# A mirrored hidden sum made on VectorE instead of by two more matmuls

## The chip, the cores and the metric

The kernel runs on one core of a Trainium2 chip. The metric is the device time of one execution in microseconds (us); the time before is the median of three executions. A core has five engines with a queue each, and a queue is worked off in order: TensorE (PE in the profile, its weight loads PEld), VectorE (DVE), ScalarE (ACT), GpSimd (POOL) and SyncE (SP). They are tied together by semaphores only, so an instruction that waits holds up all that stands behind it on its engine.

## The reference

```
X = np.fft.fft(x, axis=1)            # x: 8 x 3008 x 256, over the sequence
X = np.fft.fft(X, axis=2).real       # over the 256 features
h = np.maximum(X.reshape(24064, 256) @ w_in, 0.0)     # w_in: 256 x 2048
out = (h * h) @ w_out                                  # w_out: 2048 x 256
```

## The kernel before

**The algebra.** The feature transform and `w_in` are multiplied once, into `gh` (128 x 3 x 2048, f16): `gh[:,0]` for the cosine rows, `gh[:,1]` for the sine rows. The sequence transform of each batch is folded by its symmetries (`fold_steps`) and multiplied with tables into `zc` and `zs` (`z_steps`, lines 520 to 587): 128 rows, one column for each frequency. With P = `gh[:,0]`ᵀ·`zc` and Q + N = `gh[:,1]`ᵀ·`zs`, the full sum P+Q+N is the hidden layer at a frequency k, and P−Q+N is the one at the mirrored frequency. N is what row 0 of `zs` adds: the sine of feature frequency 0 is zero, and that row carries the cosine row of d = 128 instead, which does not change sign. `gh[:,2]` is `gh[:,1]` times −2, with row 0 set to 0 (`turn2`, line 329), so that adding `gh[:,2]`ᵀ·`zs` to the full sum turns it into P−Q+N.

**Windows and steps.** The 8 x 1505 = 12040 frequency columns are cut into 25 windows `w` of 512 columns (the first six 240, 512, 512, 240, 512, 448, the last 360; the others 512; `w` counts from 0). Each window has 8 steps `s` of two 128-row chunks of the 2048 hidden features. A step's order in the code (lines 774 to 786) is:

1. `pq(s)`: four matmuls of 512 columns into the PSUM tile `ph` (lines 742 and 743), giving P+Q+N for both chunks;
2. `square(s, 0)`: ScalarE takes the ReLU of `ph` into `h1` (line 757), VectorE squares it into `h2` (line 759);
3. `others(s)`: side work spread over the steps. It holds 16 matmuls of 256 columns of the second layer of the window before (line 647), whose results ScalarE copies out in every odd step (line 662); fold work on VectorE, one piece a step; and the z matmuls of the windows to come (line 540) with ScalarE's copies (lines 545 and 551) and VectorE's `minus` (line 563);
4. `turn(s)`: two matmuls that add `gh[:,2]`ᵀ·`zs` to the same `ph` (line 748);
5. `square(s, 1)`: ReLU and square again, columns reversed, for the mirrored half.

PSUM is full: `ph` has two buffers of two banks, the second layer's `po` two banks, `pz` two.

**What else is where.** Six windows (w = 5, 8, 10, 13, 16, 19; `fold_at`) hold the folds of a batch: `d_even` to `odds` in steps 0 to 4, `even` in step 6, `back` in step 7, each with much VectorE work (lines 410 to 437). In them GpSimd issues the load of the next batch (lines 125 and 130, step 2), the store of the even half to DRAM (line 439, step 6) and its four reads back (lines 447 and 449, step 7), which wait for that store to land. Six windows (w = 6, 9, 12, 15, 18, 21; `late_at`) hold the `late` pieces on VectorE: `fold8` twice (line 463, steps 2 and 3) and `fold16` twice (line 474, steps 4 and 5). Batch columns begin at such places that z matmuls lie in the windows 4, 6, 7, 9, 10, 11, 13, 14, 16, 17, 19, 20 and 22. The order on every engine is the order of the code: `manual_schedule` (line 98).

Of the kernel before, what the change touches and what calls it, by code (L numbers as in the profile page):

```python
# [7 lines left out]

F32 = mybir.dt.float32
F16 = mybir.dt.float16  # L10
I32 = mybir.dt.int32
AF = mybir.ActivationFunctionType
ALU = mybir.AluOpType

HS = 32.0
P = 128
# [12 lines left out]
def kernel(  # L29
# [14 lines left out]
    nc = tc.nc  # L44
    B, S, D = x.shape
    _, F = moe_w_in.shape
# [7 lines left out]
    NFC = F // P  # L54
    WN = 512
# [7 lines left out]
    NE = E + 1  # L63
# [15 lines left out]
    NW = len(wins)  # L79
# [25 lines left out]
    zp = ctx.enter_context(tc.tile_pool(name="zp", bufs=4))  # L105
    h1p = ctx.enter_context(tc.tile_pool(name="h1p", bufs=3))
    h2p = ctx.enter_context(tc.tile_pool(name="h2p", bufs=2))
    osp = ctx.enter_context(tc.tile_pool(name="osp", bufs=3))
    drp = ctx.enter_context(tc.tile_pool(name="drp", bufs=2, space=bass.MemoryType.DRAM))
    ps_h = ctx.enter_context(tc.tile_pool(name="ps_h", bufs=2, space=bass.MemoryType.PSUM))  # L110
# [43 lines left out]
    def iota(shape, pattern, base, mult, name):  # L154
        t = const.tile(shape, I32, name=name)
        nc.gpsimd.iota(t, pattern=pattern, base=base, channel_multiplier=mult)
        return t
# [9 lines left out]
        idx["r"] = iota([P, 1], [[1, 1]], P - 1, -1, "idx_r")  # L167

    xs = {0: load_x(0, idx_first)}
    w16 = [const.tile([P, 2, F // 2], F16, name=f"w16_{i}") for i in range(2)]  # L170
    for i in range(2):
        nc.gpsimd.dma_start(out=w16[i], in_=moe_w_in[:, i * F // 2 : (i + 1) * F // 2].rearrange("(c p) f -> p c f", p=P))
    wout16 = const.tile([P, NFC, D], F16, name="wout16")
# [4 lines left out]
    perm = [const.tile([P, P], F16, name=f"perm{i}") for i in range(2)]  # L178
    for i in (1, 0):
        nc.gpsimd.tensor_scalar(out=perm[i], in0=prow_i, scalar1=float(P - 1 - i), scalar2=None, op0=ALU.is_equal)  # L180
    evec_i = iota([P, 2], [[1, 2]], 0, 2, "evec_i")
    idx["c"] = iota([P, 1], [[1, 1]], P - 1, -1, "idx_c")
    nc.gpsimd.memset(idx["c"][0:2, :], P - 3)
# [39 lines left out]
    def table_steps(e):  # L223
# [17 lines left out]
                i += cnt  # L241

        def args(h):
            t = st["t", h] = tmp.tile([P, 3, NE], F32, name="t", tag="tt")
            for j in range(nr):
                r = row(h, j)
                if e == 0:
                    nc.scalar.activation(t[:, j, 0:n], st["kf"], AF.Copy, bias=R23, scale=vs[:, r : r + 1])
                else:
                    nc.vector.tensor_scalar(out=t[:, j, 0:n], in0=st["kf"], scalar1=vs[:, r : r + 1], scalar2=R23, op0=ALU.mult, op1=ALU.add)  # L250
# [237 lines left out]

    def gh_scale(out, pg, act):
        if act:  # L490
            nc.scalar.activation(out, pg, AF.Copy, bias=0.0, scale=1.0 / HS)
        else:
            nc.vector.tensor_scalar(out=out, in0=pg, scalar1=1.0 / HS, scalar2=None, op0=ALU.mult)  # L493

    def gh_step(cc, act=None):

# [11 lines left out]
    def gh_turn(cc):  # L508
        f0 = cc * 512
        nc.vector.tensor_scalar(out=gh[:, 2, f0 : f0 + 512], in0=gh[:, 1, f0 : f0 + 512], scalar1=turn2[:, 0:1], scalar2=None, op0=ALU.mult)  # L510

    zc, zs = {}, {}

# [172 lines left out]
    for i in range(2, B):  # L686
        fold_at[win_of(col_of[i, 0]) - 2] = i
        late_at[win_of(col_of[i, 1]) - 2] = i
    NST = NFC // 2
    old = None  # L690
    for w in range(NW):
        g0, wn = wins[w]
# [45 lines left out]
        def pq(s):  # L738
            ph = phs[s] = ps_h.tile([P, 2, 512], F32, name="ph", tag="psh")
            for a in range(2):  # L740
                f0 = (2 * s + a) * P
                nc.tensor.matmul(ph[:, a, 0:wn], gh[:, 0, f0 : f0 + P], zcw[:, 0:wn], start=True, stop=False)  # L742
                nc.tensor.matmul(ph[:, a, 0:wn], gh[:, 1, f0 : f0 + P], zsw[:, 0:wn], start=False, stop=True)  # L743

        def turn(s):
            for a in range(2):
                f0 = (2 * s + a) * P
                nc.tensor.matmul(phs[s][:, a, 0:wn], gh[:, 2, f0 : f0 + P], zsw[:, 0:wn], start=False, stop=True, skip_group_check=True)  # L748

        def square(s, sg):  # L750
            h1 = h1p.tile([P, 2, 512], F16, name="h1", tag="h1")
            if w == 1 and not sg:

                for a in range(2):
                    nc.scalar.activation(h1[:, a, 0:wn], phs[s][:, a, 0:wn], AF.Relu)  # L755
            else:
                nc.scalar.activation(h1[:, :, 0:wn], phs[s][:, :, 0:wn], AF.Relu)  # L757
            hv = rev_dim(h1[:, :, 0:wn], 2) if sg else h1[:, :, 0:wn]
            nc.vector.tensor_tensor(h2[:, 2 * s : 2 * s + 2, sg * wn : (sg + 1) * wn], hv, hv, op=ALU.mult)  # L759

        def others(s):
            for j in at[s]:
                j()
            for j in spread(f2, s, NST):
                j()
            for j in post[s]:
                j()
            if s == lo:
                zl[:] = [j for zu, part, h in zj for j in zu(part, h)]
            if s >= lo:  # L770
                for j in spread(zl, s - lo, hi - lo) if s < hi else []:
                    j()

        ng = 2 if w == 0 else 1
        for s0 in range(0, NST, ng):
            ss = range(s0, s0 + ng)
            for s in ss:
                pq(s)
            for s in ss:
                square(s, 0)  # L780
            for s in ss:
                others(s)
            for s in ss:
                turn(s)
            for s in ss:
                square(s, 1)
        old = (w, h2)
    for j in ffn2_steps(*old, tail=True):
        j()
# [30 lines left out]
```

## Time and profile before

| | us |
|---|---|
| device time, median of 3 (641.11, 641.24, 641.28) | 641.24 |
| span of the profiled execution, first to last instruction | 639.3 |
| PE busy, 4550 instructions | 617.4 (97%) |
| ACT busy, 618 | 456.5 (71%) |
| DVE busy, 609 | 372.5 (58%) |
| POOL busy, 130 | 77.0 (12%) |

The page gives no device time for the profiled execution alone; about 1.9 us of the median lie outside its span. The busy times of the four engines are of one execution and overlap. Matmuls are pipelined: the time that one is shown with is longer than the distance to the next. The granted TensorE clock is 0.997 over the span.

### The profile page before, as it was taken

The page shows a single profiled execution, that of the slowest core. Times are in us where ns is not written, and L with a number is a line of the kernel's source. Part 1 is how long each engine was busy: PE and PEld are TensorE (multiplying, and loading weights), DVE is VectorE, ACT ScalarE, POOL GpSimd, SP SyncE. Part 2 cuts the span into 40 slices and gives each one's busy share as a digit, 9 for nine tenths or more (in the row PEclk, how much of TensorE's full clock was granted, in tenths as well). Part 3 has the DMA queues.
Part 4 walks back from the last instruction along what each step waited for, and adds up shares of the span by engine and source line. Part 5 has one row for each costly group of instructions (what it writes and reads, how often), then busy time and mean ns, then how long its engine had stood idle before and what let it go on. Part 6 is the DMA issues. An engine that isn't in the chain of part 4 may idle for free.

```text
span 639.3 us, 11596 instructions
## 1 busy us (share of the span) xinstructions
PE 617.4 (97%) x4550; PEld 439.3 (69%) x4550; DVE 372.5 (58%) x609; ACT 456.5 (71%) x618; POOL 77.0 (12%) x130
## 2 busy tenths in 40 slices
PE   5789999999999999999999999999999999999997
PEld 2456686676676767777677667776777767776786
DVE  7777755675546656745566455764558545544440
ACT  6677766876777767777777677777777777677762
POOL 8202220012000220220003100022000200000000
PEclk9999999999999999999999999999999999999999
DMA  8736321154111721631116411173111311111112
GB/s 151 116 80 139 103 90 34 32 107 127 49 34 46 162 82 34 125 112 52 36 50 120 122 35 49 40 152 87 45 26 58 108 35 37 48 44 36 49 54 66
DMA packets 36540, 47.52 MB, mean 74 GB/s; under 512 B 4231, under 2 KB 30343, under 8 KB 36487
## 3 DMA queue, kind: packets, MB, share of 16 engines
q0 software_dynamic: 9344, 22.14, 17.2%
q1 hardware_dynamic: 26915, 24.44, 12.5%
q8 instruction: 35, 0.57, 0.4%
q10 hardware_dynamic: 228, 0.21, 0.1%
q14 instruction: 18, 0.15, 0.1%
HBM read 33.63 MB, written 27.84 MB: 96 GB/s over the span
## 4 chain that ended last, share of the span: by engine, by line
PE 91%; ACT 3%; DVE 3%; issue 2%; POOL 0%; ACTq 0%; POOLq 0%; DVEq 0%
PE po L647 50%; PE ph L748 12%; PE ph L743 12%; PE ph L742 12%; PE pz L540 4%; ACT h L757 2%; PE pw L314 1%; DVE h L759 1%; ACT h L755 0%; PE pg L503 0%; DVE gh L493 0%; ACT cos L277 0%; DVE fe L410 0%; DVE fo L414 0%; ACT osb L662 0%
## 5 line engine op out<-in xcount | busy, mean ns | idle before, releaser
L757 ACT ACTIVATE h<-ph 128x1024 f16<-128x1024 f32 (+3 forms) x392 | 361.2, 975 | 85.7 <-PE ph L748 78.9
L759 DVE TENSOR_TENSOR h<-h 128x1024 f16<-128x1024 f16 (+3 forms) x400 | 262.3, 660 | 230.1 <-ACT h L757 222.9
L647 PE MATMUL po<-wout,h 128*128 128x256 f16 (+1 forms) x3024 | 361.6, 273 | 0.0
L647 PEld LDWEIGHTS <-h 128*128 128x128 f16 (+1 forms) x3024 | 296.5, 98 | 71.5
L742 PE MATMUL ph<-zc,gh 128*128 128x512 f16 (+3 forms) x400 | 146.2, 368 | 2.7 <-ACT h L757 1.3
L743 PE MATMUL ph<-zs,gh 128*128 128x512 f16 (+3 forms) x400 | 146.2, 368 | 0.9 <-DVE zs L563 0.7
L748 PE MATMUL ph<-zs,gh 128*128 128x512 f16 (+3 forms) x400 | 114.0, 367 | 5.0 <-ACT h L757 3.1
L662 ACT ACTIVATE osb<-po 128x512 f32<-128x512 f32 (+2 forms) x94 | 54.9, 587 | 59.6 <-PE po L647 54.8
L743 PEld LDWEIGHTS <-gh 128*128 128x128 f16 x400 | 39.2, 98 | 46.4 <-issue 3.8
L742 PEld LDWEIGHTS <-gh 128*128 128x128 f16 x400 | 39.3, 98 | 44.0 <-issue 2.0
L748 PEld LDWEIGHTS <-gh 128*128 128x128 f16 x400 | 37.2, 98 | 15.4 <-issue 7.9
L480 POOL COPY xy<-xy 128x2 f16<-128x2 f16 x16 | 2.5, 186 | 164.6 <-DVE xy L463 164.6
L125 POOL DMA_DIRECT2D xo<-in_x_dram x8 | 6.1, 762 | 122.7 <-DVE fo L414 112.2
L130 POOL DMA_INDIRECT xo<-in_x_dram,idx_r x15 | 18.7, 1246 | 4.5 <-issue 4.3
L545 ACT ACTIVATE es<-pz 128x376 f32<-128x376 f32 (+1 forms) x32 | 15.4, 481 | 4.4 <-PE pz L540 2.8
L449 POOL DMA_INDIRECT rb<-scr,idx_r x16 | 17.9, 1120 | 4.9 <-issue 4.9
L551 ACT ACTIVATE zs<-pz 128x376 f16<-128x376 f32 (+22 forms) x26 | 8.3, 362 | 9.7 <-PE pz L540 9.7
L314 PE MATMUL pw<-spn 128*128 128x384 f16 x32 | 7.8, 409 | 6.7 <-DVE spn L308 6.7
L563 DVE SCALAR_TENSOR_TENSOR zc<-es,pz 128x376 f16<-128x376 f32 (+22 forms) x27 | 9.4, 383 | 7.3 <-ACT zc L551 7.3
L563 DVE SCALAR_TENSOR_TENSOR zs<-es,pz 128x376 f16<-128x376 f32 (+22 forms) x27 | 9.4, 383 | 7.1 <-ACT zs L551 7.1
L439 POOL DMA_DIRECT2D scr<-ev x8 | 4.7, 589 | 70.1 <-DVE ev L437 63.0
L540 PE MATMUL pz<-sin,od 128*128 128x376 f16 x48 | 12.2, 322 | 0.6 <-ACT es L545 0.6
(116 smaller groups left out, 245.2 us busy)
## 6 DMA issues: line engine op xcount, KB each, us to landing
out_dram<-osb SPq DMA_DIRECT2D x77, 128.0 KB
xo<-in_x_dram POOLq DMA_DIRECT2D x7, 768.0 KB, 6.7
scr<-ev POOLq DMA_DIRECT2D x8, 390.0 KB, 4.0
rb<-scr POOLq DMA_DIRECT2D x16, 130.0 KB, 2.5
out_dram<-osb SPq DMA_DIRECT2D x12, 94.0 KB
w<-in_moe_w_in_dram POOLq DMA_DIRECT2D x2, 512.0 KB
wout<-in_moe_w_out_dram POOLq DMA_DIRECT2D x1, 1024.0 KB
out_dram<-osb SPq DMA_DIRECT2D x8, 75.0 KB
```

The costliest lines, as they stand in the source:

```text
L130: nc.gpsimd.indirect_dma_start(out=flat(q), out_offset=None, in_=bass.AP(tensor=x.tensor, offset=0, ap=[[XW, B * S * D // XW], [1, XW]]), ...
L449: nc.gpsimd.indirect_dma_start(out=rb[:, q].rearrange("p r d -> p (r d)"), out_offset=None, in_=bass.AP(tensor=src.tensor, offset=src.offs ...
L540: nc.tensor.matmul(ps[:, o0:o1], lhs, tab, start=(h == 0 and k == 0), stop=last, skip_group_check=True)
L545: nc.scalar.activation(es[:, 0:n], ps[:, 0:n], AF.Copy, bias=0.0, scale=1.0)
L563: nc.vector.scalar_tensor_tensor(out=zwin(w)[part][:, o : o + cnt], in0=es[:, a : a + cnt], scalar=2.0, in1=ps[:, a : a + cnt], op0=ALU.mu ...
L647: nc.tensor.matmul(po[0:m, j * D : (j + 1) * D], h2[:, fc, q : q + m], wout16[:, fc, :], start=(fc == 0), stop=(fc == NFC - 1))
L662: nc.scalar.activation(osb[0:mm].rearrange("p s d -> p (s d)")[:, lo:hi], po[0:mm, lo:hi], AF.Copy, bias=0.0, scale=HS * HS)
L742: nc.tensor.matmul(ph[:, a, 0:wn], gh[:, 0, f0 : f0 + P], zcw[:, 0:wn], start=True, stop=False)
L743: nc.tensor.matmul(ph[:, a, 0:wn], gh[:, 1, f0 : f0 + P], zsw[:, 0:wn], start=False, stop=True)
L748: nc.tensor.matmul(phs[s][:, a, 0:wn], gh[:, 2, f0 : f0 + P], zsw[:, 0:wn], start=False, stop=True, skip_group_check=True)
L757: nc.scalar.activation(h1[:, :, 0:wn], phs[s][:, :, 0:wn], AF.Relu)
L759: nc.vector.tensor_tensor(h2[:, 2 * s : 2 * s + 2, sg * wn : (sg + 1) * wn], hv, hv, op=ALU.mult)
```

## The change

- The scale of `gh` changes its sign, and ReLU gets the scale −1, so `ph` now holds the negated sums.
- From w = 4 on some steps are made in another way: steps 2, 4 and 6, or step 5 alone in windows with folds. There `cosines` makes −P alone (two matmuls), `twice` has VectorE compute `t2` = −2·`ph` + 2N = 2P + 2N into SBUF, `sines` adds −(Q+N) (two matmuls, after `others`), ScalarE takes the ReLU of the full sum as before, and VectorE makes the mirrored half as max(`t2` + `ph`, 0) with a custom instruction (`TENSOR_ADD_SAT`). `turn` and ScalarE's second ReLU fall away in these steps.
- 2N is made once a window. In step 0 a matmul with `sel` (a matrix with ones in row 0) copies row 0 of `zsw` to all 128 partitions (`spread_nyq`), ScalarE copies it to `zn`, and GpSimd multiplies it with a column of `g2n` for each chunk: two instructions of 128x512, f32, a step so made (`nyq_rows`). The tiles `n2` take the two buffers that held `w_in`.
- `g2n` (−2 times row 0 of `gh[:,1]`, one column a chunk) comes from 16 matmuls of one column at the end of window 0 (`gh_nyq`). Four memsets for `sel` and `pick` join GpSimd's queue at the start.
- VectorE's square of a step's mirrored half is issued one step later (`kept`), behind the next step's `twice`.

```diff
-    w16 = [const.tile([P, 2, F // 2], F16, name=f"w16_{i}") for i in range(2)]
+    w16 = [wp.tile([P, 2, F // 2], F16, name=f"w16_{i}", tag="w16") for i in range(2)]
...
+    sel = const.tile([P, P], F16, name="sel")
+    nc.gpsimd.memset(sel, 0.0)
+    nc.gpsimd.memset(sel[0:1, :], 1.0)
+    pick = const.tile([P, 1], F16, name="pick")
+    nc.gpsimd.memset(pick, 0.0)
+    nc.gpsimd.memset(pick[0:1, :], -2.0)
...
-            nc.scalar.activation(out, pg, AF.Copy, bias=0.0, scale=1.0 / HS)
+            nc.scalar.activation(out, pg, AF.Copy, bias=0.0, scale=-1.0 / HS)
...
+    def gh_nyq():
+        pn = ps_o.tile([P, 512], F32, name="pn", tag="po")
+        for fc in range(NFC):
+            nc.tensor.matmul(pn[:, fc : fc + 1], gh[:, 1, fc * P : (fc + 1) * P], pick, start=True, stop=True)
+        nc.vector.tensor_copy(g2n, pn[:, 0:NFC])
...
+    diff = {w: (5,) if w in fold_at else (2, 4, 6) for w in range(4, NW)}
...
+        def spread_nyq():
+            pn = ps_z.tile([P, 512], F32, name="pn", tag="pz")
+            nc.tensor.matmul(pn[:, 0:wn], sel, zsw[:, 0:wn], start=True, stop=True)
+            zn = n2s["zn"] = znp.tile([P, WN], F16, name="zn", tag="zn")
+            nc.scalar.activation(zn[:, 0:wn], pn[:, 0:wn], AF.Copy, bias=0.0, scale=1.0)
+            for s in diff[w]:
+                nyq_rows(s)
+
+        def nyq_rows(s):
+            n2 = n2s[s] = wp.tile([P, 2, WN], F32, name="n2", tag="w16")
+            for a in range(2):
+                fc = 2 * s + a
+                nc.gpsimd.tensor_scalar(out=n2[:, a, 0:wn], in0=n2s["zn"][:, 0:wn], scalar1=g2n[:, fc : fc + 1], scalar2=None, op0=ALU.mult)
+
+        def cosines(s):
+            ph = phs[s] = ps_h.tile([P, 2, 512], F32, name="ph", tag="psh")
+            for a in range(2):
+                f0 = (2 * s + a) * P
+                nc.tensor.matmul(ph[:, a, 0:wn], gh[:, 0, f0 : f0 + P], zcw[:, 0:wn], start=True, stop=True)
+
+        def twice(s):
+            t2 = t2s[s] = tmp.tile([P, 3 * NE], F32, name="t2", tag="tt")[:, 0 : 2 * WN].rearrange("p (a n) -> p a n", a=2)
+            nc.vector.scalar_tensor_tensor(out=t2[:, :, 0:wn], in0=phs[s][:, :, 0:wn], scalar=-2.0, in1=n2s[s][:, :, 0:wn], op0=ALU.mult, op1=ALU.add)
+
+        def sines(s):
+            for a in range(2):
+                f0 = (2 * s + a) * P
+                nc.tensor.matmul(phs[s][:, a, 0:wn], gh[:, 1, f0 : f0 + P], zsw[:, 0:wn], start=False, stop=True, skip_group_check=True)
...
-        def square(s, sg):
+        def relu(s, sg):
...
+            elif sg and s in t2s:
+                nc.vector._custom_dve(TENSOR_ADD_SAT, out=h1[:, :, 0:wn], in0=t2s[s][:, :, 0:wn], in1=phs[s][:, :, 0:wn], s0=BIG, s1=0.0)
             else:
-                nc.scalar.activation(h1[:, :, 0:wn], phs[s][:, :, 0:wn], AF.Relu)
+                nc.scalar.activation(h1[:, :, 0:wn], phs[s][:, :, 0:wn], AF.Relu, bias=0.0, scale=-1.0)
+            return h1
+
+        def power(s, sg, h1):
             hv = rev_dim(h1[:, :, 0:wn], 2) if sg else h1[:, :, 0:wn]
             nc.vector.tensor_tensor(h2[:, 2 * s : 2 * s + 2, sg * wn : (sg + 1) * wn], hv, hv, op=ALU.mult)
...
+            if s0 in diff.get(w, ()):
+                cosines(s0)
+                twice(s0)
+                if kept:
+                    power(*kept)
+                others(s0)
+                sines(s0)
+                h1a = relu(s0, 0)
+                h1b = relu(s0, 1)
+                power(s0, 0, h1a)
+                kept = (s0, 1, h1b)
+            else:
+                for s in ss:
+                    pq(s)
+                if kept:
+                    power(*kept)
+                for s in ss:
+                    square(s, 0)
+                for s in ss:
+                    others(s)
+                if s0 == 0 and w in diff:
+                    spread_nyq()
+                for s in ss:
+                    turn(s)
+                if w == 0:
+                    for s in ss:
+                        square(s, 1)
+                    kept = None
+                else:
+                    kept = (s0, 1, relu(s0, 1))
+        if kept:
+            power(*kept)
+        if w == 0:
+            gh_nyq()
```

In the text below a step made in the new way is called a D step, the others N steps.

## The prediction

> **What bounds the kernel now.** The busy table of the page comes first: PE is busy 97% of the span. The timeline of one plain step then shows what such a PE is made of, here from one `turn` to the next (start, length, engine, line):
>
> ```profile
> 303.05 0.59 PE L748 MATMUL ph<-zs,gh 128*128 128x512 f16 x2
> 303.48 0.38 PE L742 MATMUL ph<-zc,gh 128*128 128x512 f16 x1
> 303.68 1.94 ACT L757 ACTIVATE h<-ph 128x1024 f16<-128x1024 f32 x2 [1.04 <-PE ph L748]
> 303.70 0.38 PE L743 MATMUL ph<-zs,gh 128*128 128x512 f16 x1
> 304.35 1.91 PE L647 MATMUL po<-wout,h 128*128 128x256 f16 x16
> 306.09 0.59 PE L748 MATMUL ph<-zs,gh 128*128 128x512 f16 x2
> ```
>
> PE has no gap: a 512-column matmul takes 0.214 us from start to start (303.48 to 303.70), the 16 of the second layer 1.74, the step 3.04. ScalarE begins 0.20 after `turn`'s last slot ends (303.48) and finishes its two ReLUs at 305.62, 0.47 before the next `turn`. So PE time taken out is time won, unless one of these cycles gets longer than PE's. What the new cycle is made of is in the groups by form (count | busy, mean ns | idle before):
>
> ```profile
> L757 ACT ACTIVATE h<-ph 128x1024 f16<-128x1024 f32 x328 | 319.1, 1026 | 71.0 <-PE ph L748 68.7 <-PE ph L743 1.2 <-issue 0.4
> L759 DVE TENSOR_TENSOR h<-h 128x1024 f16<-128x1024 f16 x336 | 231.5, 692 | 203.2 <-ACT h L757 199.3 <-issue 2.0 <-ACT h L755 1.9
> L493 DVE TENSOR_SCALAR gh<-pg 128x1024 f16<-128x1024 f32 x2 | 2.4, 1220 | 1.7 <-PE pg L503 1.7
> L563 DVE SCALAR_TENSOR_TENSOR zs<-es,pz 128x376 f16<-128x376 f32 x5 | 2.7, 540 | 0.0
> ```
>
> Two 1024-column squares back to back take 1.29 (timeline at 329.64), 0.61 each. GpSimd's own timeline, in the window that starts at 426.47, right after a fold window:
>
> ```profile
> 424.30 0.59 POOL L439 DMA_DIRECT2D scr<-ev  x1 [2.31 <-DVE ev L437]
> 431.77 1.09 POOL L447 DMA_DIRECT2D rb<-scr  x2 [6.88 <-DMA scr<-ev]
> 433.16 0.99 POOL L449 DMA_INDIRECT rb<-scr,idx_r  x1 [0.30 <-issue]
> 434.46 1.48 POOL L449 DMA_INDIRECT rb<-scr,idx_r  x1 [0.31 <-issue]
> ```
>
> The queue is stuck until 435.94, 9.47 into the window, behind a store that has not landed. Two more pairs bear on prices: VectorE against ScalarE on one PSUM tile, and GpSimd beside VectorE.
>
> ```profile
> 242.18 0.48 ACT L551 ACTIVATE zc<-pz 128x376 f16<-128x376 f32 x1
> 242.69 0.61 DVE L563 SCALAR_TENSOR_TENSOR zc<-es,pz 128x133 f16<-128x133 f32 x2 [0.61 <-ACT zc L551]
> ...
> 12.40 1.77 DVE L386 TENSOR_TENSOR u<-xo 128x3072 f16<-128x3072 f16 x1
> 12.69 1.57 POOL L215 TENSOR_SCALAR wge<-evec 128x2 f32<-128x2 f32 x1
> ```
>
> **PE's own sum.** Windows 4 to 24 are 15 without folds (45 D steps) and 6 with (6 D steps). A D step loses two matmuls of L748: 0.427 us at 512 columns, 51 of them with the narrower windows 5 and 24 make −21.3. The `sel` matmul adds 0.214 in 21 windows: +4.4. `gh_nyq` adds 16 matmuls of one column, each with a weight load (98 ns in its rows): up to 1.6; the L430/L431 pairs follow one another at 0.03, so at least 0.5. PE is followed by ScalarE there without slack, so I take 1.3. GpSimd's four memsets stand ahead of L206 and L207, whose result ScalarE's L287 awaits for 1.05 us in the head, and L287 leads to the cosine table on the chain that ends last: short GpSimd instructions there take 0.1 to 0.3 each (0.2 to 1.2 in all); I take 0.45.
>
> **The wait for 2N in windows after a fold.** `nyq_rows` stands in GpSimd's queue behind the four reads of `back`, and `twice` in step 2 waits for it; behind `twice` on VectorE wait all squares, and PE waits with `sines`. The last L449 ends 7.64, 5.07, 8.22, 8.92, 9.47 and 5.07 us into the windows 6, 9, 11, 14, 17 and 20. Against the window they come later still: L437, which L439 waits for, stands behind the longer VectorE work of D step 5 (some 0.3 by the cycle below), and the window starts up to 0.43 sooner after the batch load of step 2, since step 5 is shorter; I take 0.35. A 128x512 GpSimd product is not in the trace. From below: 128x377 of IOTA, 0.48, so 0.59 at its slope. From above: L180, 0.84 for 128 columns, 2.7 for 512. But GpSimd was held up there: L215 needs 1.57 us for two columns and ends 0.10 after VectorE's two-input L386, and L216 to L218 end likewise. Counted from the end of the VectorE instruction before it (9.06), the first L180 took 0.41; L212 took 0.24 for two columns undisturbed. That is 1.35 ns a column, 0.93 us for 512, and I take it, for VectorE is idle while it waits here. So `twice` has its input at the L449 time + 0.35 + 1.86, and takes 1.21 (L493's 1.22 for 1024 columns, L563's slope), and 0.05 to release PE. Without a wait `sines` of step 2 would start 9.25 into these windows: step 2 begins at 6.56 in the window at 426.47 (its third pair of L742 at 433.03), `sel` adds 0.21, `cosines` 0.43, side work 1.74 and two z matmuls 0.31. Waits: 1.84, 2.42, 3.12 and 3.67 in windows 6, 11, 14, 17, none in 9 and 20: +11.1. In other windows `zn` is there at 3.65 and 2N at about 5.6, before `twice` can start at 6.85: no wait. The third pair of products waits on GpSimd for `twice` of step 2 to free its buffer, and is done by 12 at the latest, when step 4's turn is not over; behind it in the queue stand only the copies of L480 to L482 (12.6 into late windows), for z matmuls a window on.
>
> The Trainium skill, "GPSIMD Engine Reference", section on elementwise cycle accounting, has 769 ns for a tight loop over 512 elements; by that, called an estimate, the sum would be 1.3 lower. No row here has the shape.
>
> **VectorE's new cycle.** Let the last `sines` slot end at 0. ScalarE's ReLU runs 0.20 to 1.23. Does the new VectorE instruction wait for it? Both read one PSUM tile. In 20 of 32 cases L563 starts 0.032 after ScalarE's read of the same tile ends, though its only input from ScalarE was copied long before (the lines above: 242.66, then 242.69). Those pairs also write parts of one z tile, which leaves a doubt; I take the wait. Then VectorE: the new instruction 1.26 to 2.48 (L493's 1.22; its program is not in the trace; below that only if it had a faster mode, which L493's PSUM input does not show), three squares (this step's two, the next step's first) to 4.24, then the next `twice` to 5.45, and PE at 5.50. PE gets there by itself at 5.22: `pq` 0.86, side work 1.74, `turn` 0.43, `cosines` 0.43, side work 1.74. So each D step that comes two after another waits 0.28, more by VectorE's side work in the N step between, less by z matmuls. Steps 4 and 6: window 23 0.56, 24 0.4. Windows 12, 15, 18, 21: `fold8` (0.62) and `fold16` (0.35) more, 1.5 each, 6.1 in all, which is above the 1.07 that PE saves in such a window. Windows 6 and 9, the same with z matmuls of 0.31 a step: 1.16 each. Windows 11, 14, 17, 20, `minus` ahead of step 6: 0.25 each. Window 4 0.6, windows 7 and 22 0.1 each. Sum +11.2. Fold windows have N steps on both sides of their D step: none. Bounds: 0 without the wait for ScalarE; 0.48 instead of 0.28 in all 30 steps, +6, if the custom instruction is 0.2 dearer.
>
> VectorE squares and GpSimd products also meet. Rows show GpSimd waiting; the other way L254, begun inside the second L180, took 1.02 instead of 0.94. I take +1.0 for the 9 windows without a wait (0 to 3.6: a square kept back by a whole product, 0.4 left over at `twice` in each). The Trainium skill, "SBUF — State Buffer", section on who interferes with whom, gives the shared ports to whichever starts first for a whole instruction, which is the upper end; the rows bear out GpSimd's side of it, hardly VectorE's.
>
> ScalarE loses 51 ReLUs (1.03) and gains 21 copies (0.60, L662's size): no cost, as it is busy 17.46 us in a 24.33 us window (300.44 to 324.77). The copy holds back step 0's second ReLU by 0.1, and step 1's `turn` has 0.4 to spare. Signs are free, in the same instructions; `kept` leaves VectorE's order in N steps as it was.
>
> Sum: −21.3 + 4.4 + 1.3 + 0.45 + 11.1 + 11.2 + 1.0 = +8.15. The profiled span 639.3 becomes 647.4; with the 1.9 that the median 641.24 has above it, **649.4**.
>
> **Rivals.**
> - *VectorE need not wait for ScalarE's read.* Then the new instruction starts at 0.2, `twice` is free at 3.2 and PE never waits in steps 4 and 6: the 11.2 goes, 638.2, faster. For it: L563 pairs share a written tile too. It decides once this cycle costs under 3.0 in all.
> - *2N is ready after folds*, the store landing early as in windows 9 and 20 (5.07): the 11.1 goes, 638.3. Against: the four late windows wait for a store queued with the next batch's load, which is untouched.
> - *Both*: 627.1.
> - *GpSimd at L180's pace*, 2.7 a product, two of them 3.5 more: waits of 25.1 in the four windows, 2.85 each in 9 and 20, 2.6 in the other nine: 692. It decides the other way below 0.6, where all else is kept, only to 646.7. Against: the held-up L215 to L218.
> - *Squares kept back by products*, each by a whole one, at the upper end of 3.6 worked out above: 652.
>
> **How the numbers follow.** Chances: forecast 0.55 (own range 642 to 658: GpSimd at 0.59 to 1.35 gives −2.7 to +3.4, the cycle ±6), first rival 0.17, second 0.10, both 0.05, GpSimd slow 0.08, ports 0.05. A measurement here tells 0.2% (1.3 us) from no change. Faster: 0.12 of the first rival, 0.07 of the second, 0.05, and 0.03 from the forecast's low end: 0.27. Same 0.05. Slower 0.68. The range 633 to 661 leaves out "both", the slow GpSimd and some tail.
>
> **What would show it.** L748's count falls by 102; PE idles before `sines` in step 2 of windows 6, 11, 14, 17 by 2 to 4 us, released by `twice`, itself by GpSimd; the custom instruction starts 0.03 after ScalarE's ReLU of its step ends; PE idles some 0.3 to 0.9 before `sines` of steps 4 and 6 in windows 12, 15, 18, 21. It is wrong if the custom instruction starts beside the ReLU, if GpSimd's products are far from 0.93, or if they stand ahead of `back` in the queue.

## The result, and the profile after

| | before | after |
|---|---|---|
| device time, median | 641.17 (641.03 to 641.28, 4 runs) | 668.17 (666.9 to 670.18, 4 runs) |
| span of the profiled execution | 639.3 | 667.1 |
| granted TensorE clock over that span | 0.997 | 0.981 |
| device time of that execution of after | | 669.2 |

The ratio is 1.0425, with a 95% interval from 1.0411 to 1.044. The kernel is slower, as forecast, but by 27.0 us and not by 8.2, and the time is above the range.

The busy table and the chain that ended last, from the page of after:

```profile
PE 613.9 (92%) x4485; PEld 435.2 (65%) x4485; DVE 485.4 (73%) x712; ACT 422.8 (63%) x588; POOL 260.9 (39%) x236
...
PE 44%; DVE 19%; issue 13%; POOL 11%; ACT 6%; DMA 6%; ACTq 0%; POOLq 0%; DVEq 0%
```

PE's busy time fell by only 3.5 us instead of some 16, although it has fewer matmuls; much of the difference is the lower clock. The rest of the span is idle time, and VectorE and GpSimd stand on the chain. The groups (busy, mean ns of one, idle before and its releaser) say which instructions:

```profile
L780 POOL TENSOR_SCALAR n<-zn,g2n 128x512 f32<-128x512 f16 (+2 forms) x102 | 184.3, 1823 | 177.6 <-ACT zn L772 177.4
...
L809 DVE CUSTOM_DVE_ANT_0 h<-t,ph 128x1024 f16<-128x1024 f32 x47 | 57.4, 1221 | 43.9 <-ACT h L811 43.9
...
L790 DVE SCALAR_TENSOR_TENSOR t<-ph,n 128x1024 f32<-128x1024 f32 (+2 forms) x51 | 61.1, 1198 | 35.4 <-POOL n L780 29.4
L795 PE MATMUL ph<-zs,gh 128*128 128x512 f16 (+2 forms) x102 | 31.0, 386 | 31.4 <-DVE t L790 31.2
```

L780 is the GpSimd product: 1.82 us, where the prediction had 0.93. L809 is the custom instruction, L790 `twice`, L795 `sines`. Read from the bottom, PE idled 31.4 us before `sines`, nearly all released by `twice`, and VectorE idled 29.4 before `twice`, released by the product. The view of waits counts them (total, times, longest):

```profile
DVE h L809 <- ACT h L811: 49.1, 51, 1.7
...
PE ph L795 <- DVE t L790: 31.2, 24, 4.7
DVE t L790 <- POOL n L780: 29.4, 6, 6.5
```

Six waits for the product: one in each of the windows 6, 9, 11, 14, 17 and 20, right after a fold window. Window 17 (it starts at 446.83) in the timeline; L456 and L458 are the reads of `back`, L762 is `pq`, L665 the second layer:

```profile
452.81 1.10 POOL L456 DMA_DIRECT2D rb<-scr  x2 [6.08 <-DMA scr<-ev]
...
454.22 1.01 POOL L458 DMA_INDIRECT rb<-scr,idx_r  x1 [0.30 <-issue]
455.53 0.98 POOL L458 DMA_INDIRECT rb<-scr,idx_r  x1 [0.30 <-issue]
...
456.55 10.34 POOL L780 TENSOR_SCALAR n<-zn,g2n 128x512 f32<-128x512 f16 x6
459.71 1.22 DVE L790 SCALAR_TENSOR_TENSOR t<-ph,n 128x1024 f32<-128x1024 f32 x1 [6.47 <-POOL n L780]
...
460.98 0.99 PE L795 MATMUL ph<-zs,gh 128*128 128x512 f16 x2 [4.71 <-DVE t L790]
...
461.77 0.63 PE L762 MATMUL ph<-zc,gh 128*128 128x512 f16 x1
...
463.47 2.39 PE L665 MATMUL po<-wout,h 128*128 128x256 f16 x16
```

The chain of the prediction is there link by link: the landed store, the last read of `back` (ends 456.51), two products, `twice`, `sines`. But the two products take 3.16 us (456.55 to 459.71). And what follows is slow too: `pq` has 0.63 instead of 0.38 a matmul. The view by stretches (columns: stretch, its length, busy time of PE, PEld, DVE, ACT and POOL, granted clock, DMA share, GB/s) shows why, here for windows 4, 6 and 17:

```profile
116.00:119.70 3.70, 1.41 (x9) 0.69 (x8) 3.58 (x6) 1.07 (x2) 2.37 (x3) 1.00 0.18 55
119.70:123.20 3.50, 3.50 (x19) 2.33 (x17) 2.82 (x4) 2.16 (x3) 0.31 (x2) 0.51 0.02 5
...
160.00:164.10 4.10, 0.58 (x5) 0.29 (x4) 1.33 (x2) 0.00 (x0) 4.10 (x3) 1.00 0.32 76
164.10:167.50 3.40, 3.40 (x11) 1.51 (x11) 2.63 (x4) 1.72 (x2) 3.40 (x3) 0.50 0.07 26
...
456.00:461.00 5.00, 0.29 (x3) 0.06 (x2) 1.29 (x2) 0.00 (x0) 4.97 (x4) 1.00 0.35 94
461.00:464.60 3.60, 3.60 (x12) 1.69 (x12) 2.25 (x3) 1.91 (x2) 3.60 (x3) 0.53 0.02 5
```

After each stretch in which PE did little, the granted clock is half for about 3.4 us. In the run before it is half only near the start and at the end.

Set side by side from one step's first matmul to the next, the two traces give the whole difference of the spans:

| place | predicted | measured |
|---|---|---|
| windows 6, 9, 11, 14, 17, 20 (after folds) | +8.0 | +22.7 |
| window 4 | −0.5 | +3.1 |
| windows 12, 15, 18, 21 | +1.8 | +3.3 |
| windows 7, 22, 23, 24 | −2.8 | −2.3 |
| fold windows | −1.3 | −1.3 |
| head, windows 0 and 1 | +1.8 | +1.4 |
| squares and products, not placed | +1.0 | |
| after the last step's start | 0 | +0.9 |
| sum | +8 | +27.8 |

The predicted column is the prediction's terms added by window: −0.43 for a D step, +0.21 for `sel`, and the waits named there.

### The profile page after: what moved, and what is told of

Same layout as the page of the kernel before. It is cut to its first block, busy times and chain, and to the rows that moved or that the text cites. A ratio compares the mean times of both kernels' runs of the same rounds, so it can differ in the third digit from the quotient of the medians.

```text
span 667.1 us, 11672 instructions
## 1 busy us (share of the span) xinstructions
PE 613.9 (92%) x4485; PEld 435.2 (65%) x4485; DVE 485.4 (73%) x712; ACT 422.8 (63%) x588; POOL 260.9 (39%) x236
## 4 chain that ended last, share of the span: by engine, by line
PE 44%; DVE 19%; issue 13%; POOL 11%; ACT 6%; DMA 6%; ACTq 0%; POOLq 0%; DVEq 0%
PE po L665 24%; DVE h L816 6%; ACT h L811 5%; DVE t L790 4%; PE ph L763 4%; PE ph L762 4%; DMA scr<-ev 4%; PE ph L800 4%; PE ph L795 4%; POOL n L780 4%; DVE h L809 3%; POOL xo L133 2%; POOL rb L458 2%; PE pz L558 2%; DVE fo L423 2%
## 5 line engine op out<-in xcount | busy, mean ns | idle before, releaser
L811 ACT ACTIVATE h<-ph 128x1024 f16<-128x1024 f32 (+3 forms) x341 | 315.6, 968 | 117.9 <-PE ph L795 86.6
L665 PE MATMUL po<-wout,h 128*128 128x256 f16 (+1 forms) x3024 | 365.1, 274 | 0.0
L665 PEld LDWEIGHTS <-h 128*128 128x128 f16 (+1 forms) x3024 | 298.7, 99 | 74.7 <-issue 3.2
L780 POOL TENSOR_SCALAR n<-zn,g2n 128x512 f32<-128x512 f16 (+2 forms) x102 | 184.3, 1823 | 177.6 <-ACT zn L772 177.4
L762 PE MATMUL ph<-zc,gh 128*128 128x512 f16 (+3 forms) x298 | 110.3, 373 | 2.5 <-ACT h L811 1.1
L763 PE MATMUL ph<-zs,gh 128*128 128x512 f16 (+3 forms) x298 | 110.7, 375 | 0.9 <-DVE zs L581 0.7
L809 DVE CUSTOM_DVE_ANT_0 h<-t,ph 128x1024 f16<-128x1024 f32 x47 | 57.4, 1221 | 43.9 <-ACT h L811 43.9
L800 PE MATMUL ph<-zs,gh 128*128 128x512 f16 (+3 forms) x298 | 84.5, 366 | 3.8 <-ACT h L811 2.3
L790 DVE SCALAR_TENSOR_TENSOR t<-ph,n 128x1024 f32<-128x1024 f32 (+2 forms) x51 | 61.1, 1198 | 35.4 <-POOL n L780 29.4
L795 PE MATMUL ph<-zs,gh 128*128 128x512 f16 (+2 forms) x102 | 31.0, 386 | 31.4 <-DVE t L790 31.2
L763 PEld LDWEIGHTS <-gh 128*128 128x128 f16 x298 | 29.6, 99 | 35.7 <-issue 5.5
L762 PEld LDWEIGHTS <-gh 128*128 128x128 f16 x298 | 29.6, 99 | 33.7 <-issue 3.9
L800 PEld LDWEIGHTS <-gh 128*128 128x128 f16 x298 | 28.2, 98 | 13.1 <-issue 6.1
L795 PEld LDWEIGHTS <-gh 128*128 128x128 f16 x102 | 9.3, 97 | 38.7 <-issue 37.1
L786 PE MATMUL ph<-zc,gh 128*128 128x512 f16 (+2 forms) x102 | 29.9, 375 | 0.0
L772 ACT ACTIVATE zn<-pn 128x512 f16<-128x512 f32 (+2 forms) x21 | 12.4, 589 | 18.9 <-PE pn L770 18.8
L456 POOL DMA_DIRECT2D rb<-scr x16 | 8.8, 557 | 28.9 <-DMA scr<-ev 28.2
```

The source lines that it names most:

```text
L665: nc.tensor.matmul(po[0:m, j * D : (j + 1) * D], h2[:, fc, q : q + m], wout16[:, fc, :], start=(fc == 0), stop=(fc == NFC - 1))
L780: nc.gpsimd.tensor_scalar(out=n2[:, a, 0:wn], in0=n2s["zn"][:, 0:wn], scalar1=g2n[:, fc : fc + 1], scalar2=None, op0=ALU.mult)
L790: nc.vector.scalar_tensor_tensor(out=t2[:, :, 0:wn], in0=phs[s][:, :, 0:wn], scalar=-2.0, in1=n2s[s][:, :, 0:wn], op0=ALU.mult, op1=ALU.add)
L795: nc.tensor.matmul(phs[s][:, a, 0:wn], gh[:, 1, f0 : f0 + P], zsw[:, 0:wn], start=False, stop=True, skip_group_check=True)
L809: nc.vector._custom_dve(TENSOR_ADD_SAT, out=h1[:, :, 0:wn], in0=t2s[s][:, :, 0:wn], in1=phs[s][:, :, 0:wn], s0=BIG, s1=0.0)
```

## The experiments

| run | median, us (range) | ratio to before, 95% interval |
|---|---|---|
| e1, 2N made once | 636.33 (636.07 to 637.28) | 0.993 [0.9913, 0.9946] |
| e2, e1 with the halves crossed | 658.51 (657.8 to 658.7) | 1.0273 [1.0256, 1.0291] |
| e3, `back` behind the products | 648.79 (648.46 to 649.11) | 1.0124 [1.0107, 1.0141] |
| e4, 2N by ScalarE | 640.28 (639.23 to 641.5) | 0.9986 [0.9974, 0.9998] |
| e5, e1 with VectorE first | 631.69 (630.73 to 632.44) | 0.9849 [0.9827, 0.987] |
| e6, 2N by ScalarE, VectorE first | 634.02 (632.87 to 635.38) | 0.9893 [0.9868, 0.9918] |
| e7, e4 with two D steps a window | 635.1 (634.95 to 635.92) | 0.9909 [0.989, 0.9928] |
| e8, forms of the product | 664.9 (one run) | |
| e9, e6 with SyncE's stores in the tail | 631.39 (631.01 to 631.91) | 0.9853 [0.9836, 0.9869] |
| e10, e6 without D steps in window 4 | 630.43 (629.25 to 631.48) | 0.9836 [0.9814, 0.9858] |
| e11, e9 and e10 together | 629.98 (629.47 to 631.24) | 0.983 [0.9813, 0.9847] |

**e1: what do GpSimd's products cost in all?**

```diff
-            for s in diff[w]:
-                nyq_rows(s)
+            if w == 4:
+                nyq_rows(2)
+                once["n2"] = n2s[2]
...
-            nc.vector.scalar_tensor_tensor(out=t2[:, :, 0:wn], in0=phs[s][:, :, 0:wn], scalar=-2.0, in1=n2s[s][:, :, 0:wn], op0=ALU.mult, op1=ALU.add)
+            nc.vector.scalar_tensor_tensor(out=t2[:, :, 0:wn], in0=phs[s][:, :, 0:wn], scalar=-2.0, in1=once["n2"][:, :, 0:wn], op0=ALU.mult, op1=ALU.add)
```

> The changed kernel, but GpSimd makes 2N only once, two products in window 4, and every D step adds that same tile (so 2N is that of step 2 of window 4 everywhere; all other work is kept, the sel matmul and ScalarE's copy of its row too). Theory: what was missed is GpSimd alone. Its products take 1.56 us each from start to start, not 0.93, so step 2 waits 20.9 us in the six windows after a fold, the granted clock is halved for 3.4 us after the longest of these waits, and VectorE's squares are held up beside products. With the products gone all of that goes and the prediction's other terms stay: -21.3 + 4.4 for PE, +1.3 at both places of the start, +11.2 for VectorE's cycle: about 637 us, step 4 of windows 12, 15, 18 and 21 still 0.9 over a D step without a wait, clock 0.997. Rival: VectorE's cycle is the larger part of the loss; then the time stays over 650.

It took 636.33. All waits before `sines` of step 2 are gone but one of 0.81 in window 4, where the two products are still made, and so is the halved clock behind them: windows 11, 14 and 17 stand at −0.95 against before instead of +4.5 to +5.6. What PE still waits for `twice` is this, against 31.2 above:

```profile
PE ph L797 <- DVE t L792: 10.3, 15, 1.7
```

So the products, with all that they drag behind them, cost 668.2 − 636.3 = 32 us. Of these 26.4 lie in the six windows after folds, 1.3 in window 4, 1.6 in the four `late` windows and 1.2 in windows 7, 22 and 23; the rest is the start and the tail, where single runs differ by such amounts. The remaining kernel, VectorE's cycle included, comes to the prediction's sum without GpSimd, though not in every part (see below).

**e2 and e5: does VectorE wait for ScalarE's read of the same tile, and can that be avoided?** e2 halves both reads and crosses them, so that each engine begins with its own bank:

```diff
+            for a in range(2):
+                b = 1 - a
+                nc.scalar.activation(h1a[:, a, 0:wn], phs[s][:, a, 0:wn], AF.Relu, bias=0.0, scale=-1.0)
+                nc.vector._custom_dve(TENSOR_ADD_SAT, out=h1b[:, b, 0:wn], in0=t2s[s][:, b, 0:wn], in1=phs[s][:, b, 0:wn], s0=BIG, s1=0.0)
```

> As e1 (one tile of 2N for all), and in each D step the ReLU of ScalarE and the custom instruction of VectorE are both cut by chunk and taken crosswise: ScalarE chunk 0 then 1, VectorE chunk 1 then 0. Theory: the custom instruction waits for ScalarE only since both read the same PSUM bank; crosswise VectorE begins 0.2 us after sines instead of 1.26, beside ScalarE, and ends near 1.5 instead of 2.5, so that no D step waits for twice: the 11.2 us of the cycle go, about 626 us. Rival: the wait is for the whole tile; then VectorE's first half still begins after ScalarE's last, two pieces cost 0.14 us more than one, and the time is that of e1 or 1 to 4 us above.

It took 658.51, worse than either expectation. The timeline of one D step, and the waits behind it:

```profile
305.16 0.60 ACT L821 ACTIVATE h<-ph 128x512 f16<-128x512 f32 x1 [0.23 <-PE ph L797]
...
305.79 0.69 DVE L822 CUSTOM_DVE_ANT_0 h<-t,ph 128x512 f16<-128x512 f32 x1 [0.19 <-ACT h L821]
...
306.51 0.60 ACT L821 ACTIVATE h<-ph 128x512 f16<-128x512 f32 x1 [0.76 <-DVE h L822]
...
307.14 0.69 DVE L822 CUSTOM_DVE_ANT_0 h<-t,ph 128x512 f16<-128x512 f32 x1 [0.66 <-ACT h L821]
...
308.08 0.59 PE L802 MATMUL ph<-zs,gh 128*128 128x512 f16 x2 [0.34 <-ACT h L813]
```

```profile
DVE h L822 <- ACT h L821: 65.0, 98, 1.4
...
ACT h L821 <- DVE h L822: 38.0, 51, 0.8
...
PE ph L802 <- ACT h L813: 16.6, 45, 1.3
```

Each of the four half reads waits for the one before it on the other engine. The first and second are in different banks (chunk 0, then chunk 1), the third and fourth too (chunk 1, then chunk 0). So reads by two engines are put one after another for the whole tile, not for a bank. ScalarE finishes the tile 1.95 us after its start instead of 1.03, its next ReLU is late, and `turn` of the following N step (L802) waits: +0.2 to +0.55 in the step behind a D step, and +0.9 in window 4. The Trainium skill, "PSUM — Partial Sum Buffer", section "PSUM bank collisions raise a hardware error", tells of the compiler back end that it orders accesses of two engines by bank and quadrant; here VectorE waited 98 times for a read of the other bank, 65.0 us in all.

e5 keeps whole reads and turns their order: VectorE's instruction first, ScalarE's ReLU of a D step behind its first ReLU of the next step, its square behind the next `twice`.

```diff
-                h1a = relu(s0, 0)
-                h1b = relu(s0, 1)
-                power(s0, 0, h1a)
-                kept = (s0, 1, h1b)
+                kept, rest0 = [(s0, 1, relu(s0, 1))], s0
...
+                if rest0 is not None:
+                    kept, rest0 = [(rest0, 0, relu(rest0, 0))], None
```

> As e1 (2N made once, the same tile for every D step), and the order at the end of a D step turned round: VectorE's custom instruction reads ph first, ScalarE's ReLU of that step is issued behind the next step's first ReLU, its square behind the next twice. Theory: twice was late in steps 4 and 6 since the custom instruction began 1.03 us after sines, behind ScalarE's read of the same tile (e2 shows that the wait is for the tile, not the bank); now it begins 0.2 after sines, VectorE is free for the next twice in time, and only cosines may wait up to 0.1 for the late ReLU: the 11 us of the cycle go, 626 to 629 us. Rival: the D steps are late by VectorE's total load, which the order does not change: 634 us or more.

It took 631.69, 4.6 less than e1. The groups of e1's and e5's custom instruction differ as the theory says, in the wait:

```profile
L811 DVE CUSTOM_DVE_ANT_0 h<-t,ph 128x1024 f16<-128x1024 f32 x47 | 57.1, 1215 | 4.7 <-PE ph L797 4.4
```

This is e5: idle 4.7 before it, released by PE; in e1 the view of waits has 51.6 us, all for ScalarE. Windows 12, 18 and 21 go from +0.42 in e1 to −1.02, nearly the whole saving of three D steps less `sel` (−1.07). What is left above 629 lies in window 4 (+1.56) and in the last step of windows with z matmuls (+0.15 to +0.61), in step 3 of window 6 (+0.47) and step 5 of window 15 (+0.32); the cause of these was not looked into.

**e3: is it the place in GpSimd's queue?** In windows 10, 13, 16 and 19 the reads of `back` move into step 1 of the next window, behind its products. The price of the product stays.

```diff
+            if w + 1 not in late_at:
+                at[7] = []
...
+        if w - 1 in fold_at and w not in late_at:
+            at[1] = [folds[fold_at[w - 1]]["back"]]
```

> The changed kernel with one thing moved: after the folds of windows 10, 13, 16 and 19 the four reads of back are issued in step 1 of the next window, behind that window's products, instead of in step 7 of the fold window. Theory: products stood behind a queue held by the store; now 2N of step 2 is ready at about 6.9 us into the windows 11, 14, 17 and 20, where twice can start at 7.4, so their step 2 loses its wait (4.4, 3.8, 5.2 and 1.8 us) and their step 3 the half clock (1.1, 1.7 and 1.3 us): about 649 us. Windows 6 and 9 keep theirs. Rival: step 2 is late since GpSimd or VectorE is slow there anyway; then no more than 4 us are gained.

It took 648.79. GpSimd's timeline in window 17 is now:

```profile
447.06 1.55 POOL L784 TENSOR_SCALAR n<-zn,g2n 128x512 f32<-128x512 f16 x1
448.56 1.18 POOL L456 DMA_DIRECT2D rb<-scr  x2
450.04 1.03 POOL L458 DMA_INDIRECT rb<-scr,idx_r  x1 [0.30 <-issue]
```

Windows 11, 14, 17 and 20 fall from +4.56, +4.48, +5.60 and +1.17 to −0.95 each; windows 6 and 9, left alone, are at +5.87 and +2.44 (+4.90 and +2.03 in the change). Products of the same price are thus harmless where nothing stands ahead of them; the queue behind the store is the place, the price sets the size.

**e8: what does a product cost?** In some windows another form takes the product's place: 2·`zn` by a constant in 12, f16 output in 15, a plain copy in 18, halves of 256 columns in 21, a memset in 23; so 2N is not made in 12, 18 and 23.

> The changed kernel, with another GpSimd instruction for 2N in five windows, to price the disputed instruction by itself (2N is wrong in those): window 12 an immediate instead of the column g2n, window 15 f16 instead of f32 output, window 18 a plain copy of zn, window 21 two instructions of 256 columns for each of 512, window 23 a memset. Starts of the first pair, before VectorE's squares come in, give the price; it is 1.56 us for 512 columns in the changed kernel. Theory of the prediction (a fixed 0.24 and some 1.35 ns a column, as the first L180 gave): the halves would take 0.58 each. Other reading: about 3 ns a column without much fixed cost, halves near 0.8, and copy and immediate at the same rate; if the rate is the input's or the output's type, the f16 output or the memset (0.83 ns a column in the IOTA rows) is far cheaper.

The groups by form (those that meet VectorE's two-input instructions are in the mean):

```profile
L792 POOL TENSOR_SCALAR n<-zn,g2n 128x512 f32<-128x512 f16 x64 | 118.9, 1873 | 75.7 <-ACT zn L772 75.6
...
L783 POOL TENSOR_SCALAR n<-zn,g2n 128x512 f16<-128x512 f16 x6 | 10.8, 1820 | 14.5 <-ACT zn L772 14.5
L781 POOL TENSOR_SCALAR n<-zn 128x512 f32<-128x512 f16 x6 | 8.9, 1519 | 15.7 <-ACT zn L772 15.7
...
L787 POOL TENSOR_SCALAR n<-zn,g2n 128x256 f32<-128x256 f16 x6 | 6.6, 1092 | 15.1 <-ACT zn L772 15.1
...
L785 POOL CAST n<-zn 128x512 f32<-128x512 f16 x6 | 5.2, 905 | 16.7 <-ACT zn L772 15.4 <-DVE t L802 1.3
...
L790 POOL MEMSET n<- 128x512 f32 x6 | 3.0, 524 | 16.6 <-DVE t L802 16.6
```

With VectorE quiet, one product lasts 1.56 us with either output type, 1.49 with the constant, 0.92 for 256 columns; a copy with the same cast lasts 0.61, the memset 0.52. The next one starts 0.02 to 0.06 before that time is over. From 0.92 and 1.56 a multiplication has some 0.28 fixed and 2.5 ns a column. The type is not what costs; the operation is.

**e4, e6 and e7: complete versions.** e4 moves the product to ScalarE, at the head of the step before the D step:

```diff
-                nc.gpsimd.tensor_scalar(out=n2[:, a, 0:wn], in0=n2s["zn"][:, 0:wn], scalar1=g2n[:, fc : fc + 1], scalar2=None, op0=ALU.mult)
+                nc.scalar.activation(n2[:, a, 0:wn], n2s["zn"][:, 0:wn], AF.Copy, bias=0.0, scale=g2n[:, fc : fc + 1])
...
+            if s + 1 in diff.get(w, ()):
+                nyq_rows(s + 1)
```

> The changed kernel with the products on ScalarE (Copy with g2n as its scale, 128x512, issued at the head of the side work of the step before each D step) instead of GpSimd; nothing left out. Theory: as e1, about 637 us, if ScalarE's spare time (6.9 us a window before the change, 3.1 more by the ReLUs taken over) covers six products of about 0.6 us. Rival: ScalarE, which a step's turn waits for, becomes the bound in N steps before D steps (two ReLUs, two products and a copy of results, 1.84 + 1.0 + 0.5, against a step of 3.04): 0.3 us a step, 45 steps, about 650 us.

e6 is e4 with e5's order; the products of the later D steps stand in the D step before:

```diff
+            if w in diff and s + 1 == diff[w][0]:
+                nyq_rows(s + 1)
...
+                if s0 + 2 in diff[w]:
+                    nyq_rows(s0 + 2)
```

> Both repairs in a complete kernel: the products on ScalarE (for step 2 in step 1, for steps 4 and 6 in the D step before) and the custom instruction ahead of ScalarE's ReLU as in e5. Theory: as e5, plus some tenths where ScalarE's products meet its other work: 627 to 632 us, below the kernel before. Rival: ScalarE's products make its ReLUs late for turn: 636 or more.

e7 is e4 with other D steps:

```diff
-    diff = {w: (5,) if w in fold_at else (2, 4, 6) for w in range(4, NW)}
+    diff = {w: (5,) if w in fold_at else (2, 5) for w in range(4, NW)}
```

> The products on ScalarE as in e4, order as in the changed kernel, but only two D steps, 2 and 5, in windows without folds, so that two N steps lie between them. Theory: twice is late only where a D step comes two steps after another; with two N steps between, no D step waits. PE saves 36 D steps: -15.0 + 4.4, start +1.7, about 632 us. Rival: a D step waits by itself, whatever is in front: then fewer D steps save less and the time stays at e4's 640.

e4 took 640.28, e6 634.02, e7 635.1: each faster than the change, each 2 to 3 above what was expected. The steps were nearly as expected. In e4 windows 11, 14, 17 and 20 are at −0.83, and all six windows after folds are as in e1 within 0.12; in e7 D steps wait in windows 4, 7 and 22 and in fold windows with z matmuls alone, and a plain window gains 0.65; in e6 windows 12, 15, 18 and 21 gain 1.02. The missing part came after the last step began: 20.3 to 20.5 us to the end, where before has 17.6 and the change 18.5. e4's timeline there (ACTq are ScalarE's DMA issues), and the last line of its chain:

```profile
628.81 0.38 ACT L669 ACTIVATE osb<-po 128x256 f32<-128x256 f32 x1 [1.36 <-PE po L665]
629.23 4.24 ACTq L645 DMA_DIRECT2D out_dram<-osb  x2
633.59 0.65 ACT L669 ACTIVATE osb<-po 128x256 f32<-128x256 f32 x2 [4.39 <-issue]
```

```profile
629.23 3.95 ACTq L645
```

In before the same two issues of an output store take 0.81. With them at 4.24, ScalarE's last copies come late. These three kernels show it (4.24, 4.26 and 4.24); before, the change and the five other runs above do not.

**e9, e10 and e11: the slow issue, and window 4.** e9 gives these stores to SyncE, e10 leaves the issues but starts the D steps at window 5, e11 does both.

```diff
-                    store(osb[:, 0, :], nu, g0 + 2 * wn - q - m, m - nu, True, nc.scalar if i % 2 else nc.sync)
+                    store(osb[:, 0, :], nu, g0 + 2 * wn - q - m, m - nu, True)
```

> The kernel with 2N from ScalarE and VectorE's half first, and the three output stores that ScalarE issues in the tail now issued by SyncE. With 2N on ScalarE, the first of those issues took 3.95 us instead of some 0.4, ScalarE's copies of the last results and so the end waited behind it, and the tail from the start of the last step was 20.3 to 20.5 us instead of 17.7. Theory (that issue is the whole of the longer tail, 2.7 us): 634.0 - 2.7 = 631.3, up to 632.3 if SyncE's own queue of stores ends up to 1 us later for the three it takes over. Rival (the stall is that of ScalarE's queue at this place whatever stands there, and meets the copy that follows): no change, 633.5 to 634.5.

```diff
-    diff = {w: (5,) if w in fold_at else (2, 4, 6) for w in range(4, NW)}
+    diff = {w: (5,) if w in fold_at else (2, 4, 6) for w in range(5, NW)}
```

> The same kernel with ScalarE's stores as they were and the first D steps in window 5: window 4, whose side work is half because window 3 has 240 columns, keeps N steps. It lost 1.33 us in that window against the kernel before; without D steps it loses nothing: 632.7. The tail's slow issue stays in theory one (it comes with this form of the kernel): 20.4 us; in theory two (it depends on how many ScalarE instructions stand ahead of it, here four fewer) it may move, and the time would be 630.

> Both edits. If the slow issue is gone with ScalarE's stores and window 4 loses nothing: 634.0 - 2.7 - 1.3 = 630.0 (629.5 to 631). If only window 4's part holds: 632.7.

e9 took 631.39, 2.6 less than e6, with a tail of 18.4 instead of 20.5, which is that of the change: the slow issue was what set these three tails apart from it. Why the tail of the change is 0.9 longer than before was not looked into. e10 took 630.43, and its issue is short with ScalarE's stores still in place:

```profile
620.88 1.10 ACTq L645 DMA_DIRECT2D out_dram<-osb  x2
```

ScalarE has 686 instructions there instead of 690, so the stall does not come with 2N on ScalarE as such. But e7 has 675 and shows it, so it is not the count alone, and what ScalarE waits for in it stays open. Window 4 is at 0.0 in e10, as expected. e11's 629.98 lies within e10's range: with the stall gone, who issues these stores makes no difference that shows. e10 and e11 beat both kernels: they take 1.6 and 1.7% less than the kernel before.

## Why the prediction was right in sign and wrong in size

**The step that failed** is the price of a GpSimd product, 0.93 us in the prediction and 1.56 measured, and with it the wait for 2N. Two things that the sum put at nothing came on top: the wait in windows 9 and 20, where the queue was taken to be free in time, and the half clock behind long waits.

**Right.** PE's own sum: a D step without a wait is 0.43 shorter, `sel` makes step 0 0.21 to 0.22 longer (nothing in windows 4 and 6), and the fold windows with one D step come out at −0.21. The head: +0.44 (predicted 0.45). VectorE's cycle: the custom instruction takes 1.22 and starts 0.03 after ScalarE's ReLU in 51 of 51 cases. The first rival, that it need not wait, is out as the change stands; but the wait comes from the order of the two reads in the program, and e5 shows that it can be turned for 4.6 us. The windows after folds wait in their steps 4 and 6 for 3.2 in all (predicted 3.3). Without the products the sum is 649.4 − 11.1 − 1.0 = 637.3, and e1 measured 636.3. That they are so close is in part luck: in e1 window 4 takes 2.3 more than predicted, windows 0 and 1 take 1.1 less, and the others together 1.3 less.

**Near by luck: windows 0 and 1.** They are at +0.94, where the prediction had 1.3 for the 16 matmuls of `gh_nyq`. These took 0.47 us in all, less than its lower bound of 0.5. The rest is the granted clock, which is half for 6.83 us at this place, and for 3.41 in the run before. In e1, e2 and e9, which have the same code here and a half clock of 3.41, the two windows are at +0.2; in e3, e6, e7 and e8, which have none, at −0.85.

**Wrong: the price of a product, and with it the wait for 2N.** 0.93 us was worked out from the first L180, 128 columns in 0.41, and L212. A 512-column product takes 1.56 undisturbed. The fourth rival's 2.7 was too high, so the truth lay between the prediction's two readings of L180, and the choice of the lower one failed. In the six windows step 2 is longer than a D step without a wait by this (PE's idle time alone adds up to 18.8; the rest is mostly `sines` at half clock):

| window | 6 | 9 | 11 | 14 | 17 | 20 | sum |
|---|---|---|---|---|---|---|---|
| predicted | 1.84 | 0 | 2.42 | 3.12 | 3.67 | 0 | 11.1 |
| measured | 4.05 | 1.64 | 4.42 | 3.75 | 5.23 | 1.77 | 20.9 |

The two products are 3.16 instead of 1.86, +1.3 in each window. The other part is when `back` ends: L458 ends 7.68, 6.45, 8.86, 8.55, 9.68 and 6.57 into these windows. In windows 9 and 20 that is 1.4 and 1.5 later than before, where 0.35 was taken, and it turned their slack into a wait; the store is issued 0.57 to 0.71 ahead of the window, where before it was 1.6 to 2.2, since VectorE's L446, which it waits for, now comes later. In window 14 the landing happened to be earlier than before. The Trainium skill's 769 ns ("GPSIMD Engine Reference", section "Elementwise — side-by-side cycle accounting"), which the prediction set beside its own price, is further off still: the product is twice that.

**Wrong: a term that was not there.** PE's idle stretches of 3.5 to 4.7 us in windows 6, 11, 14 and 17 halve the clock for what follows: step 3 is 1.30, 1.08, 1.68 and 1.32 longer, 5.4 us. The Trainium skill, "TensorE: Matmul & The Clock Gate", advises against PE gaps above about 3 us (section "Why this matters for your kernels") and has half rate for about 3.4 us (section "What's actually happening"); the lengths here, 3.41 each, agree. The prediction's own waits of 3.12 and 3.67 were near that size, and it should have put a price on the risk.

**Wrong: window 4.** The cycle of 5.22 that PE takes by itself contains 1.74 of side work twice. Window 3 has 240 columns, so side work in window 4 has 8 matmuls a step instead of 16, and PE arrives earlier while VectorE does not. The window also holds the `late` pieces of batch 1 on VectorE (line 746 of the kernel after), which the prediction left out: a `fold8` stands right ahead of `twice` in step 2, and ahead of that in step 4 a `fold16`, which takes 0.83 beside the products and 0.42 in e1. Before `sines` of steps 2 and 4 PE has gaps of 0.81 and 2.29 there, and the clock halves here too. Predicted −0.5, measured +3.1; e1, with the products of step 2 alone, has gaps of 0.81, 1.72 and 1.01 before steps 2, 4 and 6, no half clock and +1.8.

**Too small: squares and products.** The 1.5 taken for a `late` window is 1.9 measured (step 4 waits 1.32, step 6 0.59), and 1.5 in e1, where the products are gone. Windows 7, 22 and 23 lose 0.4 each in the same way. With the 1.3 in window 4, which holds the clock too, this is 4.1 against the 1.0 in the sum, just above its upper end of 3.6.

In one sum: 9.8 more wait for 2N, 5.4 of halved clock in the same windows, 3.6 in window 4, 1.5 in the `late` windows and 0.5 in windows 7, 22, 23 and 24 together, 0.9 in the tail, less 1.0 that had been set aside for squares and less 0.4 at the start, is 20.3; the measured time is 19.7 us of span above the predicted one. Of the 0.6 between, 0.4 lies in the six windows, whose `sel` and steps 4 and 6 cost a little less than predicted; the rest is rounding.

## What to carry to other kernels

Before an engine on the critical path is made to wait for an idle one, price that engine's instruction by a row of the same operation and width, or measure it once, and read what stands ahead of it in its queue. Moving four DMA reads behind the products (e3) or the products to another engine (e4) was worth 19 and 28 us here, against the 16 of PE time that the change itself saves. A wait of PE of some 2 us and more can have a second price behind it, the halved clock; it came behind all eight waits of 3.49 us and more. And where two engines read one PSUM tile, the one whose result is needed first should stand first in the program.

## What the runs showed of the hardware that was not expected

- A GpSimd multiplication of 128x512 takes 1.56 us, and up to 2.5 while VectorE runs two-input instructions (e3 has one of 2.52 at 416.34); one of 448 columns took 2.90 in window 5. A copy with the same cast takes 0.61. The other way, some of VectorE's squares took 0.84 to 1.17 instead of 0.69 (one 1.56), and `fold8` (L472) 845 ns in the mean instead of 694.
- Whether a gap halves the clock depends on where it falls, not on its length alone. All changes of the granted clock in a run lie on one raster of 3.413 us: in the run of the change the halved stretches begin at 30.96, 119.70, 164.08, 297.20, 379.12 and 461.04, which is 26, 13, 39, 24 and 24 raster steps apart. From window 1 to the last step, the clock turned from full to half in ten places in the traces of the change, e3 and e8, each time behind a raster step in which PE was busy for at most 0.39 of the time; the lowest share behind which it stayed full, in all traces, is 0.49 (e1, window 4). So the gap of 2.29 us in window 4 halved the clock in the change and in e3, where one raster step held most of it (0.33 and 0.39 busy), and not in e8, where two shared it (0.56 and 0.68). A gap of 2.91 in e8 (window 14) was shared so too (0.53 and 0.62) and did not halve it, nor did any gap of up to 1.81. So a part of the cost of window 4 is chance: +3.1 in the change, +2.4 in e8. In window 6 of e3 and e8 the half clock lasted two raster steps, 6.83 us.
- The issue of an output store on ScalarE took up to 3.97 us instead of 0.53, and cost 2.1 us of tail (e6 against e9) in kernels that did not touch that store. It came in three programs (e4, e6, e7) and not in e10, which has fewer D steps than e6; what ScalarE waits for is not shown.
